# Layer one's first product: eight of its twelve quads by seven half-size products, with q and k in one load, the last rows flushed one by one, and a new order

## The chip, the cores and the metric

The kernel runs on one core of one Trainium2 chip. The metric is the device time in microseconds (us): 617.07 us before, the median of three runs (616.88 to 617.26). The engines are named as the profile names them: PE multiplies matrices, PEld loads its weights, DVE is the vector engine, ACT the activation engine, POOL is GpSimd, SP issues the DMAs. An L with a number is a line of the kernel's code.

## The reference

Windowed attention is followed by two feed-forward layers, all in fp32, on 2 x 768 tokens of width 512 (8 heads of 64):

```python
# _attn_ref: local window of 96 keys, 8 global keys, slopes per head
keep = is_global | is_local
bias = -slopes[:, None, None] * dist[None, :, :]
scores = np.where(keep, scale * q @ k.T + bias, -1e9)
a = np.exp(scores - max); a = a / (a.sum() + 1e-9); x = a @ v
# _moe_ref: layer one, d_ff 2048
g = s * np.maximum(x @ w_in, 0.0) ** 2 + b;  x = g @ w_out
# _moe2_ref: layer two, d_ff 2048
g = np.maximum(x @ w_in, 0.0) ** 2;          out = g @ w_out
```

## The kernel before

**Precision.** Every large matrix is kept as a high and a low part, so a product is three matmuls: high by high, high by low, low by high. Such a part of a weight block is a "unit" of 128 x 512 (name u, 30 of them). A weight block comes by DMA into a staging tile (`st`, three of each kind) in a packed 64-bit form, is decoded by four steps (one ACT copy, then L50, L52, L55 on DVE) and split into units: the high part by a copy (`copy_r`, L198 on ACT, L200 on DVE, L202 on POOL), the low part by a DVE subtraction (L416).

**Attention.** Twelve tiles n of 128 queries: q·k (L334), mask and row maximum on DVE (`ttr`, L342), exponent on ACT (`exp`, L350), sums and scaling, transposes (L367) that ACT or DVE copies out (`at`, L373, L375), product with v (L388), and the result split into `xh` (ACT) and `xl` (DVE). q, k and v come by one load each and tile (`load`). Until the first h, `warm` puts small matmuls (L299, L301) on PE where it would idle.

**The layers.** A layer's 2048 hidden columns are 16 blocks of 128. Layer one's first four blocks run on pieces of 256 tokens while attention still goes on (`h` L643 and `y` L722). All other blocks go in pairs a, a+1 over halves tp of 768 tokens; a pair and a half is a "quad". Layer one has twelve quads (a = 4, 6, ..., 14, two halves), layer two sixteen (a = 16, ..., 30). A half has two sides of 384 tokens.

- Layer one's first product is `plain` (L506): four results (block, side) of 12 matmuls of 384 columns each, 48 for a quad.
- Layer two's first product is `product` (L496): a Strassen form. The pair of blocks and the halves of the 512 inputs make a 2 x 2 matrix of weights, the sides and the input halves a 2 x 2 matrix of x, and seven products s = 0..6 of 6 matmuls, 42 for a quad, take the place of eight. It wants sums of weights (`wsum` L433, split by L448 into units A1, S12, S34 and A22), sums of x (T1..T4: `tsum` L475, `tsplit`, L481, into `th`, `tl` and, for T1, over x's own place), and after the matmuls a copy m1 (`mid`, L198 or L200), two sums u2, u3 (L516) and three sums `cadd` (L529) on DVE that read PSUM.
- The results then pass `act`: relu (ACT L542, DVE L544), square (ACT L551), high part gh (ACT L562, L564 or POOL L566), low part gl (DVE L569 in layer one, L572 in layer two), and the second product (`y2`, L592 in layer one, L598 in layer two) adds into six PSUM banks. `flush2` (L612, L633 on DVE) adds the banks to `acc`; at the end of layer two L629 sends each row block out.

Between the layers `acc` is scaled on ACT, split again into xh, xl, and T1..T4 are formed anew. Layer two's first product waits for them.

**What sets the order.** `order` states every piece of work as a task with engines, an assumed duration, dependencies and due time, and `Plan.run` simulates them and writes each engine's instructions in that order. CFG and the table SHIFT move due times. On the chip each engine runs its row in order, so an instruction that waits holds all behind it. The product s=3 waits for u2, s=5 for u3 and s=6 for a `cadd`, all of DVE.

Of the kernel before, what the change touches and what calls it, by code (L numbers as in the profile page):

```python
# [8 lines left out]
F32 = mybir.dt.float32  # L9
# [4 lines left out]
ALU = mybir.AluOpType  # L14
# [3 lines left out]
DM = H * D  # L18
# [11 lines left out]
NUA, NUB = 20, 10  # L30
WINO1 = False
# [27 lines left out]
def decoded(a):  # L59
# [4 lines left out]
           moe=82.8, moe0=27.8, pair=8.16, patience=3.27, slow=1.1, wload=64.22, l1s=44.16, l2s=9.05, chain2=-10.14,  # L64
           ylag2=8.98, ylag=10.91, tk=13.15)
# [30 lines left out]


class Plan:
# [13 lines left out]
    def run(self, lat, patience):  # L112
# [79 lines left out]
        self.time = max(free.values())  # L192
# [12 lines left out]
class Fast:  # L205
    def __init__(self, ctx, tc, q, k, v, wi, wo, s_t, b_t, nl_t, ng_t, ident, nm, ok, out):
        self.ok, self.tc, self.nc, self.ctx = ok, tc, tc.nc, ctx
        self.q, self.k, self.v, self.wi, self.wo, self.out = q, k, v, wi, wo, out
# [36 lines left out]
    def second(self):  # L245

        self.actx.close()
        ctx = self.ctx
# [4 lines left out]
        self.psY2 = self.pool(ctx, "psY2", 1, space=bass.MemoryType.PSUM)


    def consts(self, step):
        nc, nr, far, dist, key = self.nc, self.nr, self.far, self.dist, self.key
        if step == 0:
            nc.gpsimd.iota(nr[:, 1, :], pattern=[[-1, P]], base=0, channel_multiplier=1,
                           allow_small_or_imprecise_dtypes=True)  # L260
# [8 lines left out]
            nc.gpsimd.iota(dist[:, 0, :], pattern=[[1, P]], base=-P, channel_multiplier=-1,
                           allow_small_or_imprecise_dtypes=True)  # L270
        elif step == 1:
            k = key[:, 0, :]
            nc.vector.tensor_scalar(out=far[:, 1, :], in0=nr[:, 1, :], scalar1=self.nl, scalar2=-NEG, op0=ALU.is_ge,
                                    op1=ALU.mult)
            nc.vector.tensor_scalar(out=k, in0=k, scalar1=self.ng, scalar2=-NEG, op0=ALU.is_ge, op1=ALU.mult)
            nc.vector.tensor_tensor(out=dist[:, 1, :], in0=dist[:, 1, :], in1=far[:, 1, :], op=ALU.min)
            nc.vector.tensor_scalar(out=k, in0=k, scalar1=self.nl, scalar2=None, op0=ALU.subtract)
            nc.vector.tensor_tensor(out=key[:, 1, :], in0=dist[:, 1, :], in1=k, op=ALU.max)
        else:
            nc.vector.tensor_scalar(out=far[:, 0, :], in0=nr[:, 0, :], scalar1=self.nl, scalar2=-NEG, op0=ALU.is_ge,  # L280
                                    op1=ALU.mult)
            nc.vector.tensor_tensor(out=dist[:, 0, :], in0=dist[:, 0, :], in1=far[:, 0, :], op=ALU.min)
            nc.vector.tensor_copy(dist[:, 0, 0:G], key[:, 0, 0:G])
# [22 lines left out]
    def blocks(self, n):  # L306
        return slice(1 if n < 2 else 0, 2)
# [957 lines left out]
```

## Time and profile before

| | us |
|---|---|
| median of three runs | 617.07 |
| span of the profiled execution | 615.60 |
| PE busy | 601.59 |
| DVE busy | 446.70 |
| ACT busy | 345.75 |
| POOL busy | 96.85 |

The results give the medians of runs and the span of the profiled execution; the profiled execution has no device time of its own beside its span. The span is 1.47 us below the median. Busy time is a union per engine, so the instructions' own durations, which overlap a little at their ends, add up to more.

### The profile page before, as it was taken

The page shows a single profiled execution, that of the slowest core. Times are in us where ns is not written, and L with a number is a line of the kernel's source. Part 1 is how long each engine was busy: PE and PEld are TensorE (multiplying, and loading weights), DVE is VectorE, ACT ScalarE, POOL GpSimd, SP SyncE. Part 2 cuts the span into 40 slices and gives each one's busy share as a digit, 9 for nine tenths or more (in the row PEclk, how much of TensorE's full clock was granted, in tenths as well). Part 3 has the DMA queues.
Part 4 walks back from the last instruction along what each step waited for, and adds up shares of the span by engine and source line. Part 5 has one row for each costly group of instructions (what it writes and reads, how often), then busy time and mean ns, then how long its engine had stood idle before and what let it go on. Part 6 is the DMA issues. An engine that isn't in the chain of part 4 may idle for free.

```text
span 615.6 us, 10179 instructions
## 1 busy us (share of the span) xinstructions
PE 601.6 (98%) x3766; PEld 545.0 (89%) x3766; DVE 446.7 (73%) x997; ACT 345.8 (56%) x759; POOL 96.9 (16%) x167
## 2 busy tenths in 40 slices
PE   6999999999999999999999999999999999999995
PEld 4778989899999999999999888899999999998984
DVE  6888878766888684447648899878887897764542
ACT  6889886875655453334328476755555554543330
POOL 4334323121111100011103111111200101000000
PEclk9999999999999999999999999999999999999999
DMA  7765434103353330013100301322220322010113
GB/s 270 278 203 195 160 113 155 36 2 103 112 162 104 109 98 34 1 34 105 34 0 2 103 35 35 103 70 68 69 69 11 127 70 68 3 34 0 41 64 108
DMA packets 16473, 52.12 MB, mean 85 GB/s; under 512 B 2080, under 2 KB 2080, under 8 KB 16416
## 3 DMA queue, kind: packets, MB, share of 16 engines
q1 hardware_dynamic: 16416, 51.39, 25.2%
q8 instruction: 32, 0.52, 0.4%
q14 instruction: 25, 0.20, 0.1%
HBM read 48.24 MB, written 3.15 MB: 83 GB/s over the span
## 4 chain that ended last, share of the span: by engine, by line
PE 90%; DVE 4%; ACT 3%; DMA 2%; issue 0%; SPq 0%; ACTq 0%
PE yy L598 21%; PE h L496 18%; PE h L506 16%; PE yy L592 16%; PE y L722 6%; PE h L643 5%; PE a L334 3%; PE a L388 3%; PE a L367 3%; DMA st<-in_moe_w_in_dram 2%; ACT sn L350 1%; DVE sn L342 1%; DVE acc L633 1%; ACT acc L198 1%; ACT xh L198 0%
## 5 line engine op out<-in xcount | busy, mean ns | idle before, releaser
L598 PE MATMUL yy<-u,gh 128*128 128x512 f32 x384 | 119.2, 392 | 0.0
L506 PE MATMUL h<-xh,u 128*128 128x384 f32 x384 | 102.5, 337 | 0.0
L592 PE MATMUL yy<-gh,u 128*128 128x512 f32 (+1 forms) x384 | 97.5, 337 | 0.0
L598 PEld LDWEIGHTS yy<-u,gh 128*128 128x128 f32 x384 | 71.5, 188 | 12.2
L598 PE MATMUL yy<-u,gl 128*128 128x512 f32 x192 | 75.3, 392 | 0.9 <-DVE gl L572 0.9
L496 PE MATMUL h<-xh,u 128*128 128x384 f32 x256 | 75.5, 337 | 0.0
L592 PEld LDWEIGHTS yy<-gh,u 128*128 128x128 f32 x384 | 66.5, 189 | 7.9
L506 PEld LDWEIGHTS h<-xh,u 128*128 128x128 f32 x384 | 69.9, 188 | 0.4
L551 ACT ACTIVATE r<-r 128x384 f32<-128x384 f32 x80 | 41.9, 525 | 47.0 <-DVE r L544 30.6
L592 PE MATMUL yy<-gl,u 128*128 128x512 f32 (+1 forms) x192 | 64.8, 337 | 0.0
L506 PE MATMUL h<-xl,u 128*128 128x384 f32 x192 | 64.6, 337 | 0.0
L202 POOL TENSOR_SCALAR u<-st 128x512 fp32r<-128x512 f32 (+1 forms) x41 | 29.3, 715 | 222.8 <-PE h L506 103.5
L496 PE MATMUL h<-th,u 128*128 128x384 f32 x192 | 56.8, 336 | 0.0
L198 ACT ACTIVATE st<-st 128x512 f32<-128x512 f32 x64 | 42.7, 677 | 13.8 <-DMA st<-in_moe_w_in_dram 7.0
L569 DVE SCALAR_TENSOR_TENSOR gl<-r,sgb,gh 128x384 fp32r<-128x384 f32 x48 | 30.4, 635 | 25.2 <-ACT gh L562 21.1
L52 DVE SCALAR_TENSOR_TENSOR st<-st 128x512 int32<-128x512 int32 x64 | 45.6, 714 | 3.9 <-ACT st L198 0.7
L496 PEld LDWEIGHTS h<-xh,u 128*128 128x128 f32 x256 | 47.1, 188 | 1.0
L350 ACT ACTIVATE sn<-sn,nm 128x256 f32<-128x256 f32 (+1 forms) x96 | 46.0, 483 | 0.8 <-DVE nm L342 0.8
L55 DVE SCALAR_TENSOR_TENSOR st<-st 128x512 int32<-128x512 int32 x64 | 44.8, 700 | 1.0
L542 ACT ACTIVATE r<-h,rt 128x384 f32<-128x384 f32 x34 | 19.7, 580 | 43.8 <-PE h L506 43.8
L598 PEld LDWEIGHTS yy<-u,gl 128*128 128x128 f32 x192 | 36.1, 188 | 9.3 <-DVE gl L572 1.3
L496 PE MATMUL h<-xl,u 128*128 128x384 f32 x128 | 43.0, 336 | 0.0
(135 smaller groups left out, 1223.8 us busy)
## 6 DMA issues: line engine op xcount, KB each, us to landing
st<-in_moe_w_in_dram SPq DMA_DIRECT2D x32, 512.0 KB, 3.8
st<-in_moe_w_out_dram SPq DMA_DIRECT2D x32, 512.0 KB, 3.6
k<-in_k_dram SPq DMA_DIRECT2D x10, 512.0 KB, 4.9
v<-in_v_dram SPq DMA_DIRECT2D x10, 512.0 KB, 4.6
q<-in_q_dram SPq DMA_DIRECT2D x12, 256.0 KB, 4.1
out_dram<-acc SPq DMA_DIRECT2D x12, 256.0 KB, 2.6
k<-in_k_dram SPq DMA_DIRECT2D x2, 256.0 KB, 5.0
v<-in_v_dram SPq DMA_DIRECT2D x2, 256.0 KB, 7.1
```

Of the source, the lines that this page charges most:

```text
L52: nc.vector.scalar_tensor_tensor(out=lo, in0=hi, scalar=3, in1=lo, op0=ALU.logical_shift_left, op1=ALU.bitwise_or)
L55: nc.vector.scalar_tensor_tensor(out=lo, in0=hi, scalar=-(1 << 31), in1=lo, op0=ALU.bitwise_and, op1=ALU.bitwise_or)
L198: nc.scalar.activation(out=out, in_=in_, func=AF.Copy, scale=scale)
L350: self.nc.scalar.activation(out=sn[:, x], in_=sn[:, x], func=AF.Exp, scale=-1.0, bias=self.nm[:, n, h:h + 1], accum_out=self.rs[:, n, h:h ...
L496: self.nc.tensor.matmul(ps, p, q, start=first and kt == 0 and x == 0, stop=kt == 1 and x == 2, skip_group_check=not first)
L506: self.nc.tensor.matmul(ps, p[:, kt * P:(kt + 1) * P], self.X[q][:, kt, lo:lo + SB], start=(kt == 0 and x == 0), stop=(kt == KT - 1 and x ...
L551: nc.scalar.activation(out=r, in_=r, func=AF.Square)
L569: nc.vector.scalar_tensor_tensor(out=gl, in0=r, scalar=self.sgb, in1=gh.bitcast(F32), op0=ALU.add, op1=ALU.subtract)
L592: self.nc.tensor.matmul(yj, p[:, js], q[:, lo:hi], start=first and x == 0 and not (side and j % 2), stop=last and x == 2 and not (side and ...
L598: self.nc.tensor.matmul(y[m], p[:, ms], q, start=first and x == 0, stop=last and x == 2)
L643: self.nc.tensor.matmul(ps[:, 0:hi - lo], a[:, kt * P:(kt + 1) * P], b[:, kt, lo:hi], start=(kt == 0 and x == 0), stop=(kt == KT - 1 and x ...
L722: self.nc.tensor.matmul(yj, a[:, js], b, start=first and x == 0 and j % 2 == 0, stop=last and x == 2 and j % 2 == 1)
```

## The change

- PLAIN names the four quads that keep `plain`: (4,0), (6,0), (4,1), (6,1). The eight quads of a = 8, 10, 12, 14 take `product`. Their x sums come from `tsum1`: since x is held as two parts, a T takes three or two DVE operations in place of one, 40 in all, through a tile `tq` of its own; T2..T4 go to the place that layer two uses later. T1 is written over x's own second side, so it waits until the half's plain products are done. The added weight sums, units and PSUM sums are those of layer two's quads.
- q and k of a tile lie in one tensor `qk` and come by one load. The mask's blocks are swapped to match (own keys first). There are 29 units in place of 30.
- The very last quad (30,1) computes its second product row block by row block (`yrow`): six matmuls of both blocks, then that row is added and sent; the last row in two halves of 256 columns.
- The planner's durations, its rule for DVE and POOL at once, and the SHIFT table are new, so nearly every row has moved.

```diff
-NUA, NUB = 20, 10
-WINO1 = False
+NUA, NUB = 20, 9
+PLAIN = ((4, 0), (6, 0), (4, 1), (6, 1))
...
-        if what == "q":
-            start(out=t, in_=self.q[b, i])
-        else:
-            start(out=t[:, a], in_=(self.k if what == "k" else self.v)[b, i, :, a])
+        if what == "q":
+            t = self.qp.tile([P, 3, 4, P], F32, tag="q", name=f"q{n}")
+            self.T["q", n], self.T["k", n] = t[:, 0], t[:, 1:3]
+            a = slice(0, a.stop + 1)
+            start(out=t[:, a], in_=self.qk_[b, i, :, a])
...
+    def tsum1(self, tp, kt, step):
+        nc = self.nc
+        h, l = ([x.bitcast(F32)[:, r + kt, tp * TB + c * SB:tp * TB + (c + 1) * SB] for r, c in
+                 ((0, 0), (0, 1), (2, 0), (2, 1))] for x in self.X)
+        if step in (0, 3):
+            self.T["t", tp, kt] = self.tq.tile([P, SB], F32, tag="tq", name=f"tq{step}_{tp}_{kt}")
+        t = self.T["t", tp, kt]
+        ops = {3: ((h[3], h[1]), (t, l[3]), (t, l[1])), 0: ((h[1], h[0]), (t, l[1]), (t, l[0])),
+               1: ((h[3], t), (t, l[3])), 2: ((h[2], t), (t, l[2]))}[step]
+        for x, (p, q) in enumerate(ops):
+            plus = q is l[3] or q is l[2] or step == 0 and q is l[1]
+            nc.vector.tensor_tensor(out=t, in0=p, in1=q, op=ALU.add if plus else ALU.subtract)
...
+    def yrow(self, a, tp, m):
+        y = self.T["y", tp]
+        ms = slice(m % 3 * P, (m % 3 + 1) * P)
+        for c in range(2):
+            gh, gl = (t[:, self.T["g", a, tp, c, m // 3]][:, ms] for t in self.G)
+            oh, ol = (self.T[x, a + c, 1] for x in ("wh", "wl"))
+            for x, (p, q) in enumerate(((gh, oh), (gh, ol), (gl, oh))):
+                self.nc.tensor.matmul(y[m], p, q, start=False, stop=c == 1 and x == 2)
...
-    wino = lambda a: a >= NCH or WINO1
+    plain = lambda a, tp: (a, tp) in PLAIN
...
+    for tp in range(2):
+        d0 = ["second"] + [("h", w, lo) for w in range(NF) for lo in range(tp * TB, tp * TB + TB, 256)]
+        d1 = [("p", a, tp, c, x) for a, t in PLAIN if t == tp for c in range(2) for x in range(2)]
...
+                add(("zsh",) + v + (x,), "ACT:0.44 POOL:0.6", lambda e, v=v, x=x: f.tsplit(*v, x, 0, e),
+                    [("zs",) + v + (x,)] + d1 * (n == 1), k)
```

SP's row at the start, before (k0, q0 are tile 0's loads, st0_0 and st1_0 block 0's first and second weights):

```order
L1201 DMA ni_62<-in_n_dram 128x4
L321 DMA k0_166<-in_k_dram 128x512
L319 DMA q0_168<-in_q_dram 128x512
L37 DMA st0_0_170<-in_moe_w_in_dram 128x1024
L319 DMA q1_172<-in_q_dram 128x512
L321 DMA k1_174<-in_k_dram 128x512
L321 DMA v0_181<-in_v_dram 128x512
L321 DMA v1_183<-in_v_dram 128x512
L1212 DMA sb_61<-in_sb_dram 128x2
L319 DMA q2_193<-in_q_dram 128x512
L37 DMA st1_0_208<-in_moe_w_out_dram 128x1024
L321 DMA k2_213<-in_k_dram 128x1024
```

The same stretch of SP's row after the change (q is now q with k):

```order
L1289 DMA ni_62<-in_n_dram 128x4
L343 DMA q0_163<-in_qk_dram 128x1024
L37 DMA st0_0_165<-in_moe_w_in_dram 128x1024
L343 DMA q1_167<-in_qk_dram 128x1024
L346 DMA v0_169<-in_v_dram 128x512
L346 DMA v1_171<-in_v_dram 128x512
L1300 DMA sb_61<-in_sb_dram 128x2
L343 DMA q2_179<-in_qk_dram 128x1536
L37 DMA st1_0_181<-in_moe_w_out_dram 128x1024
```

Tile 2's keys stood twelfth, behind block 0's second weights; they now come with its q in the eighth row, ahead of them.

DVE's row while PE works on quad (8,0)'s first product, before (st is a weight block being decoded, gl a low part, yy the banks of quads 4 and 6 of the second half):

```order
L612 TENSOR_TENSOR acc_118<-yy3_4_1_2701,acc_118 128x512
L55 SCALAR_TENSOR_TENSOR st1_14_2850<-st1_14_2850 128x512
L50 TENSOR_SCALAR st1_15_2874<-st1_15_2874 128x512
L52 SCALAR_TENSOR_TENSOR st1_15_2874<-st1_15_2874 128x512
L569 SCALAR_TENSOR_TENSOR gl_106<-r8_0_00_2941,sgb_121,gh_105 128x384
L55 SCALAR_TENSOR_TENSOR st1_15_2874<-st1_15_2874 128x512
L612 TENSOR_TENSOR acc_118<-yy4_4_1_2702,acc_118 128x2x256
```

The same place after the change (tq3_1_1 is a sum for T3 of the second half):

```order
L523 TENSOR_TENSOR tl_1983<-tq0_1_0_2778,th_1982 128x384
L559 TENSOR_TENSOR u2_8_0_2913<-h8_0_1_2896,m1_8_0_2903 128x384
L517 TENSOR_TENSOR tq3_1_1_2915<-xh_116 128x384
L517 TENSOR_TENSOR tq3_1_1_2915<-tq3_1_1_2915,xl_117 128x384 x2
L559 TENSOR_TENSOR u3_8_0_2935<-h8_0_1_2896,m1_8_0_2903 128x384
L52 SCALAR_TENSOR_TENSOR st1_12_2844<-st1_12_2844 128x512
L572 TENSOR_TENSOR u3_8_0_2935<-h8_0_2_2928,u3_8_0_2935 128x384
L612 SCALAR_TENSOR_TENSOR gl_106<-r8_0_00_2925,sgb_121,gh_105 128x384
L572 TENSOR_TENSOR r8_0_10_2961<-h8_0_1_2896,m1_8_0_2903 128x384
```

Where DVE had only decoding and low parts, PE's next products now stand behind u2, u3 and the sums, with three tq operations between u2 and u3 and a decode step (L52) ahead of the first L572.

PE's last nine matmuls before (yy3 to yy5 are the last three row blocks; u28 and u29 one block's weights, the other block's matmuls stand earlier):

```order
L598 MATMUL yy3_28_1_6041<-u28_2117,gh_105 128x512
L598 MATMUL yy3_28_1_6041<-u29_2118,gh_105 128x512
L598 MATMUL yy3_28_1_6041<-u28_2117,gl_106 128x512
L598 MATMUL yy4_28_1_6042<-u28_2117,gh_105 128x512
L598 MATMUL yy4_28_1_6042<-u29_2118,gh_105 128x512
L598 MATMUL yy4_28_1_6042<-u28_2117,gl_106 128x512
L598 MATMUL yy5_28_1_6043<-u28_2117,gh_105 128x512
L598 MATMUL yy5_28_1_6043<-u29_2118,gh_105 128x512
L598 MATMUL yy5_28_1_6043<-u28_2117,gl_106 128x512
```

And after the change (u15 and u16 are one block's weights, u17 and u18 the other's):

```order
L650 MATMUL yy4_28_1_6153<-u15_97,gh_105 128x512
L650 MATMUL yy4_28_1_6153<-u16_98,gh_105 128x512
L650 MATMUL yy4_28_1_6153<-u15_97,gl_106 128x512
L650 MATMUL yy4_28_1_6153<-u17_99,gh_105 128x512
L650 MATMUL yy4_28_1_6153<-u18_100,gh_105 128x512
L650 MATMUL yy4_28_1_6153<-u17_99,gl_106 128x512
L650 MATMUL yy5_28_1_6154<-u15_97,gh_105 128x512
L650 MATMUL yy5_28_1_6154<-u16_98,gh_105 128x512
L650 MATMUL yy5_28_1_6154<-u15_97,gl_106 128x512
L650 MATMUL yy5_28_1_6154<-u17_99,gh_105 128x512
L650 MATMUL yy5_28_1_6154<-u18_100,gh_105 128x512
L650 MATMUL yy5_28_1_6154<-u17_99,gl_106 128x512
```

A row block was finished every three matmuls at the end; it is now finished every six.

Counted over the whole of both orders: PE's matmuls of 384 columns go from 1248 to 1200 (L506: 576 to 192; by seven products: 672 to 1008), the warming ones of 256 columns (L301) from 61 to 48; attention's last product with v has 240 h and 204 y matmuls ahead of it before and 228 and 144 after. DVE gains 40 `tsum1` operations, 16 low parts of them, 16 u2 and u3, 24 `cadd`, 16 weight sums, one more large and one more small weight low part for each of four pairs, and 8 more m1 copies; it loses 10 relus and 8 `at` copies, which go to ACT. POOL has 20 more rows.

## Rows read from the trace of the kernel before

**Rows 1.** The page: busy us of each engine, its share of the span, instructions.
```profile
PE 601.6 (98%) x3766; PEld 545.0 (89%) x3766; DVE 446.7 (73%) x997; ACT 345.8 (56%) x759; POOL 96.9 (16%) x167
```

**Rows 2.** Busy time by stage: width, then each engine's busy time, clock, DMA.
```profile
6.00:28.00 22.00, 18.35 (x169) 14.07 (x167) 17.45 (x92) 18.95 (x71) 8.45 (x21) 1.00 0.91 339
...
42.00:140.00 98.00, 98.00 (x918) 88.25 (x920) 76.47 (x246) 79.38 (x231) 29.08 (x50) 1.00 0.34 114
140.00:352.00 212.00, 212.00 (x1262) 200.04 (x1258) 144.32 (x254) 105.55 (x183) 26.55 (x35) 1.00 0.23 73
352.00:376.00 24.00, 23.13 (x128) 21.16 (x127) 22.45 (x41) 14.18 (x24) 2.57 (x5) 1.00 0.06 23
376.00:608.00 232.00, 232.00 (x1159) 208.93 (x1157) 169.35 (x311) 115.27 (x218) 22.78 (x36) 1.00 0.18 57
```

**Rows 3.** Chain of waits: start, length, engine, tile, line, matmuls.
```profile
45.79 2.85 PE h L643 x24
...
177.63 4.16 PE h L506 x24
...
485.86 1.04 PE h L496 x6
```

**Rows 4.** DVE's groups by form: count, busy us, mean ns, idle before and releaser.
```profile
L516 DVE TENSOR_TENSOR u<-h,m 128x384 f32<-128x384 f32 x32 | 17.8, 556 | 12.6 <-PE h L496 11.4 <-ACT m L198 1.1
...
L448 DVE TENSOR_TENSOR u<-st,u 128x512 fp32r<-128x512 f32 x24 | 16.8, 703 | 1.2 <-ACT u L198 0.7 <-POOL u L202 0.5
...
L375 DVE COPY at<-a 128x512 f32<-128x512 f32 x16 | 11.0, 687 | 8.2 <-PE a L367 8.1
L433 DVE TENSOR_TENSOR st<-st,st 128x256 f32<-128x256 f32 x24 | 10.5, 469 | 0.1
...
L544 DVE TENSOR_SCALAR r<-h,rt 128x384 f32<-128x384 f32 x14 | 8.7, 619 | 24.8 <-PE h L506 24.8
...
L475 DVE TENSOR_TENSOR t<-acc,t 128x384 f32<-128x384 f32 x8 | 4.8, 594 | 0.3
...
L448 DVE TENSOR_TENSOR u<-st,u 128x256 fp32r<-128x256 f32 x8 | 3.3, 417 | 0.2 <-ACT u L198 0.2
...
L200 DVE TENSOR_SCALAR m<-h 128x384 f32<-128x384 f32 x3 | 1.7, 558 | 4.4 <-PE h L496 4.4
```

**Rows 5.** DVE's timeline early in layer two: start, length, line, tile.
```profile
382.09 0.55 DVE L572 TENSOR_TENSOR gl<-u,gh 128x384 fp32r<-128x384 f32 x1
382.56 0.55 DVE L475 TENSOR_TENSOR t<-acc 128x384 f32<-128x384 f32 x1
```

**Rows 6.** POOL's timeline around layer one's end, with idle before.
```profile
331.95 1.01 POOL L566 TENSOR_SCALAR gh<-r,sgb 128x384 fp32r<-128x384 f32 x1 [1.51 <-ACT r L551]
...
350.76 0.59 POOL L566 TENSOR_SCALAR gh<-r,sgb 128x384 fp32r<-128x384 f32 x1 [2.00 <-ACT r L551]
```

**Rows 7.** SP's timeline of the opening: the keys of tiles 1 and 2.
```profile
3.14 0.43 SPq L321 DMA_DIRECT2D k<-in_k_dram  x1
...
8.70 0.33 SPq L321 DMA_DIRECT2D k<-in_k_dram  x1
```

**Rows 8.** PE's timeline of the opening: the second tile's q·k.
```profile
10.06 1.16 PE L334 MATMUL a<-k,q 64*128 64x128 f32 x16 [2.11 <-DMA k<-in_k_dram]
```

**Rows 9.** Timeline of the last 12 us.
```profile
604.94 4.13 DVE L633 TENSOR_TENSOR acc<-yy,acc 128x512 f32<-128x512 f32 x6 [6.17 <-PE yy L598]
...
605.66 3.92 SPq L629 DMA_DIRECT2D out_dram<-acc  x6
...
607.95 0.40 PE L598 MATMUL yy<-u,gl 128*128 128x512 f32 x1
```

**Rows 10.** DMA view of 600 to 616 us: KB each, median us to landing.
```profile
out_dram<-acc SPq DMA_DIRECT2D x6, 256.0 KB, 3.7
```

**Rows 11.** The page: a costly group of PE, and the DMA issues of the whole run.
```profile
L598 PE MATMUL yy<-u,gl 128*128 128x512 f32 x192 | 75.3, 392 | 0.9 <-DVE gl L572 0.9
...
out_dram<-acc SPq DMA_DIRECT2D x12, 256.0 KB, 2.6
```

More of the change, by code (lines that the diff above doesn't have):

```diff
@@ L170, in run @@
                     if e == "POOL" or e == "DVE" and self.port[t]:
-                        free[e] = max(now, held["DVE" if e == "POOL" else "POOL"]) + engs[e]
+                        free[e] = now + 0.4 * max(0.0, held["DVE" if e == "POOL" else "POOL"] - now) + engs[e]
                         held[e] = free[e]
@@ L191, in run @@
                 now = max(now, heapq.heappop(events))
-        self.time = max(free.values())
+        self.time = max(max(free.values()), queue + 1.2)
 def copy_r(nc, eng, out, in_, scale=1.0):
@@ L783, in order @@
         key = vt[n, 0] - LEAD - 8 if two else -40 + n
-        for what in "qk":
-            add(("l" + what, n), "SP:0.47",
-                lambda e, a=(what, n): f.load(*a), [], -900.0 + 2 * n if not two else key,
-                acq=[(what, n)], dma=0.73 * (2 if two and what == "k" else 1))
+        add(("lq", n), "SP:0.47", lambda e, n=n: f.load("q", n), [], -900.0 + 2 * n if not two else key,
+            acq=[("q", n)], dma=2.2 if two else 1.46)
         add(("lv", n), "SP:0.47", lambda e, n=n: f.load("v", n), [("lv", n - 1)] * (n > 0),
@@ L797, in order @@
                     dq.append(("tr", m, grp(m, mf)[0]))
-                add(("qk",) + u, {"PE": 1.06}, lambda e, u=u: f.qk(*u), dq, t, acq=[("a", "s", x) + u for x in range(2)],
-                    rel=[("q", n), ("k", n)] * (hf or not two))
+                add(("qk",) + u, {"PE": 1.07 if two else 1.17}, lambda e, u=u: f.qk(*u), dq, t, acq=[("a", "s", x) + u for x in range(2)],
+                    rel=[("q", n)] * (hf or not two))
             su = u if two else (n, 0)
@@ L846, in order @@
                 t += L1S if a < NCH else L2S
-    wino = lambda a: a >= NCH or WINO1
+    plain = lambda a, tp: (a, tp) in PLAIN
+    pure = lambda a: plain(a, 0) and plain(a, 1)
+    mixed = lambda a: plain(a, 0) != plain(a, 1)
     at, nu = {}, 0
@@ L856, in order @@
     for a in range(NF, 2 * NCH, 2):
-        if wino(a):
-            for what in ("A1", "S12", "S34"):
+        if not pure(a):
+            for what in ("A1", "A2", "S12", "S34") if mixed(a) else ("A1", "S12", "S34"):
                 for x in "hl":
@@ L861, in order @@
                     nu += 1
-            at["A22", a] = nu
-            nu += 1
+            if not mixed(a):
+                at["A22", a] = nu
+                nu += 1
             parts = [(a, 1), (a + 1, 1)]
@@ L876, in split @@
         u, v = at[w, i, "h"], at[w, i, "l"]
-        add(("whi", w, i), "ACT:0.58 POOL:0.62", lambda e: f.whi(w, i, e, u), [("d3", w, i)] + late(w, i, "h"), key,
+        add(("whi", w, i), "ACT:0.6 POOL:0.66", lambda e: f.whi(w, i, e, u), [("d3", w, i)] + late(w, i, "h"), key,
             acq=[slot(w, i, "h")])
@@ L889, in parts @@
             dd = [d] + ([("ws", a, 2)] if what == "S34" else [])
-            add(("wsh", what, a), "ACT:0.33 POOL:0.35" if small else "ACT:0.58 POOL:0.62",
+            add(("wsh", what, a), "ACT:0.35 POOL:0.38" if small else "ACT:0.6 POOL:0.66",
                 lambda e, what=what, k=at[ka]: f.wshi(a, what, e, k), dd + late(*ka), key, acq=[slot(*ka)])
@@ L951, in order @@
         span = L1S if one else L2S
-        dt = ["second"] if one else [("tsl", tp, kt, x) for kt in range(2) for x in range(4)] + [
-            ("xl", "x", tp, j) for j in (0, 2, 3)]
+        if not one:
+            dt = [("tsl", tp, kt, x) for kt in range(2) for x in range(4)] + [("xl", "x", tp, j) for j in (0, 2, 3)]
+        elif plain(a, tp):
+            dt = ["second"]
+        else:
+            dt = [("zsl", tp, kt, x) for kt in range(2) for x in range(4)]
+        wino = not plain(a, tp)
         blocks = {(0, 0): 2, (1, 1): 5, (1, 0): 5, (0, 1): 6}
-        if wino(a):
-            need = (["A1"], ["S12"], ["A1"], ["S34"], ["S12"], ["A22"], ["S34"])
+        if wino:
+            a22 = "A2" if mixed(a) else "A22"
+            need = (["A1"], ["S12"], ["A1"], ["S34"], ["S12"], [a22], ["S34"])
             extra = ([], [], [("m1",) + u], [("u2",) + u], [], [("u3",) + u], [("cadd",) + u + (1, 1)])
@@ L978, in order @@
                 v = u + (c, side)
-                add(("p",) + v, {"PE": 2.1}, lambda e, v=v: f.plain(*v), [prev, ("wlo", a + c, 0)] + dt * (x == 0),
+                add(("p",) + v, {"PE": 2.09}, lambda e, v=v: f.plain(*v),
+                    [prev, ("wsl", "A2" if c else "A1", a) if mixed(a) else ("wlo", a + c, 0)] + dt * (x == 0),
                     tm + 2.1 * x, acq=[("h",) + v],
-                    rel=[slot(a + c, 0, k) for k in "hl"] * (gone and side))
+                    rel=[slot(a + c, 0, k) for k in "hl"] if gone and side and not mixed(a) else [])
@@ new lines, in order @@
+            if wino and (c, side) != (0, 0):
+                add(("relu",) + v, "ACT:0.56", lambda e, v=v: f.act(*v, "relu", e), [("cadd",) + v], k)
+            else:
+                pre = ("p",) + (u + (2,) if wino else v)
+                add(("relu",) + v, "ACT:0.6 DVE:0.52", lambda e, v=v: f.act(*v, "relu", e), [pre, "sq"], k,
+                    acq=[("r",) + v], rel=[("h",) + u + (0,) if wino else ("h",) + v])
+            add(("sq",) + v, "ACT:0.53", lambda e, v=v: f.act(*v, "sq", e), [("relu",) + v], k)
@@ L996, in order @@
+            fg = (c, side) in ((0, 0), (1, 1) if wino else (1, 0))
+            add(("gh",) + v, "ACT:0.53 POOL:0.72" if one else "ACT:0.44 POOL:0.6", lambda e, v=v: f.act(*v, "gh", e),
+                [("sq",) + v] + ([] if fg or not one else [("gh",) + u + ((0, 0) if c == 0 else (1, 1) if wino else (1, 0))]),
                 k, acq=[("g",) + u + (c, x) for x in range(2)] * fg if one else [("g",) + v])
-            add(("gl",) + v, "DVX:0.53" if one else "DVX:0.47", lambda e, v=v: f.act(*v, "gl", e), [("gh",) + v], k,
+            add(("gl",) + v, "DVX:0.56" if one else "DVX:0.49", lambda e, v=v: f.act(*v, "gl", e), [("gh",) + v], k,
```

217 lines of the change are left out of this document (121 added, 96 removed), and 53 rows, old and new, of the table SHIFT.

## The prediction

> **What bounds the kernel now.** I read the busy times first: PE is busy for 601.6 us of 615.6, DVE for 446.7 [rows 1]. Then the busy times by stage, since an average says little about a kernel with stages. From 42 to 140 us (attention with layer one's first blocks), from 140 to 352 (the rest of layer one) and from 376 to 608 (layer two) PE is busy for the whole of each stretch [rows 2]. Time is lost in three places only: the opening (18.35 of 22 us from 6 to 28, part of that fill matmuls), the handover from 352 to 376 (23.13 of 24), and behind the last matmul, which starts at 607.95 in a span of 615.60 [rows 2, 9]. So a matmul taken out is worth its time on PE if the others keep up, and the question is who keeps up. The chain of waits gives the price: 24 matmuls of `plain` in 4.16 us, 6 of `product` in 1.04, both 0.173 us apiece [rows 3]. The groups' mean (337 ns and the like) is no price, since matmuls overlap.
>
> **The change, part by part.** The sum is made against the profiled execution's span, 615.60, and the differences are carried to the median of 617.07, 1.47 us above it.
>
> *Matmuls.* Eight quads go from 48 to 42, so 48 matmuls of 384 columns fall away: 48 x 0.173 = -8.3 us, on the engine that is always busy. That PE issues fewer is certain from the order (1248 to 1200); only waits can take it back.
>
> *DVE in layer one.* Added, by durations of the nearest forms [rows 4]: 40 `tsum1` operations and 16 low parts at 0.594 (33.3 us), 16 u2 and u3 and 24 `cadd` at 0.556 (22.2), 16 weight sums at 0.469 (7.5), four large and four small weight low parts at 0.703 and 0.417 (4.5), 8 copies m1 at 0.558 (4.5); taken off: 10 relus at 0.619 (6.2). Together 65.8 us in 118 more instructions. Where DVE runs back to back a 384-column operation of 0.55 us is followed 0.47 later [rows 5], so each costs 0.08 less: about 56.4 us. The stretch from 140 to 352 had 144.3 us of DVE work in 212 [rows 2], 68%. It becomes 200.7 in 203.7 (212 less 8.3), or in some 212 since the attention phase ends earlier (next part): 95 to 99%. That is the term I am least sure of. One end: in layer two, with u2, u3 and `cadd` in every quad and DVE at 73%, PE loses nothing [rows 2], so +0. The other: from 352 to 376 DVE is at 94% and PE loses 0.87 of 24 us, of which the wait for one gl (0.9) is all [rows 2, 11]; that share over 204 us is +7.4. By load the second row is nearer, but its wait is that of one chain through the rebuilding of x, which layer one doesn't have; the x sums of each half are due only when that half's first seven-product quad comes, and until then they may slip. I take +1.5. Weight units are no new limit, I think: a seven-product pair wants 11 of 29 where a plain one took 8 of 30, and layer two runs on 11 of 30 without loss.
>
> *POOL beside it.* POOL gets 20 more operations, and DVE many more with two SBUF inputs. A gh on POOL took 1.01 us at 331.95, while DVE formed the sums T, and 0.59 later [rows 6]: 0.42 more. POOL is busy 26.55 of 212 us [rows 2], so 20 x 0.42 = 8.4 us of it are hidden. The Trainium skill, "GPSIMD Engine Reference", section "8. Key points", says that GpSimd shares its SBUF interfaces with VectorE and contends with its instructions that have two SBUF inputs. The trace agrees as to POOL; whether DVE pays the same no row shows, and if it does the sum is that of the first rival.
>
> *Attention phase.* The order has 72 fewer h and y matmuls ahead of attention's last product with v (240 + 204 to 228 + 144). At 2.85/24 = 0.119 us [rows 3] PE has 8.6 us less work to spread over the same ACT and DVE work. From 42 to 140 ACT is busy 79.4 and DVE 76.5 of 98 us [rows 2]; in 89.4 that is ACT at 89% (more, with 8 `at` copies of 0.687 [rows 4] from DVE). The matmuls are not lost, only later. Bounds: 0, as now at 81%; +4, if PE idles by half of the 8.6 us. I take +0.8, towards the low end, since the tiles' chains are staggered and no row shows PE idle at 81%.
>
> *Opening.* The second tile's q·k at 10.06 waited 2.11 us for its keys, whose load was issued at 3.14 as the fifth large one [rows 7, 8]; with q and k in one load it is the third, some 0.9 us earlier. Tile 2's keys were issued only at 8.70 and now come before block 0's second weights. Against that, the queue moves 339 GB/s at a DMA share of 0.91 from 6 to 28 us, and ACT is busy 18.95 of the 22 [rows 2]: bytes and ACT bound the gain at the 3.05 us that ACT idles. The loss: one 512 KB transfer must land whole where q and k landed apart. Half of one (256 KB at 339 GB/s, 0.8 us) twice over is about +1.5. I take -1.0, the earlier issue.
>
> *Handover.* A gl that waits (0.9 [rows 11]) may stay or go; the dependencies are the same. 0, from -0.9 to +1.
>
> *Tail.* DVE's six flushes end at 604.94 + 4.13 = 609.07, 0.72 us behind PE's last matmul (607.95 + 0.40), and the six row blocks go out within 3.92 us and take 3.7 to land [rows 9, 10]; over the run the same transfer takes 2.6 [rows 11]. A row block now comes every 6 x 0.229 = 1.37 us (4.13/6 was three matmuls) so the queue is empty when the last one comes: 2.6 - 3.7 = -1.1. Halves save perhaps 0.2 in the transfer and cost one more DVE start. I take -1.0 (-1.5 to +0.3, if the low parts are late for the denser last rows).
>
> Sum: -8.3 + 1.5 + 0.8 - 1.0 + 0 - 1.0 = -8.0, that is 607.6 of span and **609.1 us**.
>
> **The rivals.**
> *DVE becomes layer one's bound.* For it: 95 to 99% by the count. If the 8.4 us of contention fall on DVE as well, it has 209.1 us of work for 203.7, and PE waits 5.4 in place of 1.5: 613.0. Against it: DVE can take weight decoding ahead in attention, where it is at 78%.
> *Attention stalls.* ACT at 89% with all chains closer: +4 in place of +0.8, 612.3.
> *Waits inside the quads eat the gain; the kernel is slower.* A plain product waits for no one. In the new quads PE's s=3, 5 and 6 each stand behind a DVE result, 24 places in layer one. Between s=1 and s=3 lies one product, 1.04 us, and u2 needs 0.556, so DVE may be 0.48 late for nothing. In the new order three tq operations (3 x 0.51 with the starts counted, 1.5 us) stand between u2 and u3 in quad (8,0), and decode steps in front of sums. If half of the 24 places find such a triple in front, PE waits 12 x (1.5 - 0.48) = 12.2 us, and it comes to 617.07 - 9.5 + 12.2 = 619.8. From 0.40 us per place on (9.5/24) the change loses. Against it: layer two has 48 such places and loses nothing [rows 2].
> *All goes well.* Opening -3.05, tail -1.5, no new waits: 617.07 - 12.9 = 604.2.
>
> **How the numbers follow.** The forecast, 606.5 to 611.5, has 0.54; all well, about 604 to 606.5, 0.14; DVE as bound 0.12 and attention stalls 0.08, both within 611.5 to 615.8; waits inside the quads 0.12, of which a third ends near 617 and the rest above. The measurement tells 0.2% (1.2 us) from no change. So faster 0.88, same 0.04, slower 0.08, and the range from 604.0 to 614.0.
>
> **What would show it.** Matmuls: 42 per quad at 0.173 us each in the chain. DVE: its busy share in the stretch from the last product with v to layer two's first, and PE's idle time there by releaser: `product` waiting for u2, u3 or `cadd` means the slower rival, y2 waiting for gl, or weights that come late, means DVE as bound. Attention: PE's idle time between 28 and 130 us, ended by ACT. Opening: the second tile's q·k before 10.06 us. Tail: some 6.2 us from the last matmul's end to the span's, which were 7.25 (615.60 - 608.35). I am wrong at the root if PE, with 48 fewer matmuls, shows more than 5 us of new idle time in layer one.

## The result, and the profile after

The changed kernel takes 607.77 us (median of four runs, 606.85 to 608.63) against 617.16 before: a ratio of 0.985 (95% interval 0.9836 to 0.9862), 9.4 us less. The profiled execution has a span of 605.10 us (its own time is 606.85) where 615.60 were, 10.5 less. The runs after spread over 1.8 us; a possible cause is in the last section.

The page's busy times of the kernel after, first part:

```profile
PE 591.4 (98%) x3705; PEld 533.9 (88%) x3705; DVE 496.8 (82%) x1115; ACT 354.5 (59%) x774; POOL 113.7 (19%) x187
```

Against [rows 1] PE has 10.2 us less (the matmuls and some fill), DVE 50.1 us more. The prediction's count gave 56.4 in layer one, less 5.5 for the `at` copies (8 at 0.687), 50.9.

Busy time by stage of the kernel after (columns as in [rows 2]):

```profile
6.00:28.00 22.00, 20.23 (x185) 15.27 (x181) 20.45 (x105) 21.62 (x78) 11.00 (x26) 1.00 0.83 337
28.00:42.00 14.00, 14.00 (x146) 11.92 (x144) 12.95 (x47) 13.65 (x44) 7.85 (x13) 1.00 0.74 244
42.00:130.00 88.00, 88.00 (x846) 79.25 (x843) 74.65 (x240) 71.19 (x204) 29.62 (x47) 1.00 0.34 112
...
140.00:340.00 200.00, 197.89 (x1155) 184.72 (x1155) 178.82 (x333) 113.85 (x201) 28.07 (x37) 1.00 0.20 64
340.00:366.00 26.00, 26.00 (x141) 23.56 (x140) 25.48 (x47) 17.43 (x30) 3.12 (x5) 1.00 0.14 41
366.00:597.50 231.50, 229.65 (x1147) 206.68 (x1147) 172.08 (x321) 107.54 (x205) 29.99 (x45) 1.00 0.19 61
```

The kernel before from 28 to 42 us, in the same view:

```profile
28.00:42.00 14.00, 13.06 (x130) 10.53 (x129) 13.38 (x46) 10.68 (x32) 5.26 (x9) 1.00 0.48 156
```

Three things are to be seen. ACT is busy for 21.62 of the opening's 22 us (it was 18.95). DVE is at 89% from 140 to 340 (layer one behind attention) and at 98% in the handover from 340 to 366; from 42 to 130 it is at 85%, where it was at 78% [rows 2]. And PE, which lost nothing between 140 and 352 before, now loses 2.1 us up to 340 and 1.9 later.

PE's waits of the kernel after, 140 to 340 us and then 340 to 400 (total, times, longest):

```profile
PE yy L635 <- DVE gl L612: 1.8, 1, 1.8
PE yy L635 <- ACT gh L605: 0.2, 1, 0.2
```
```profile
PE h L538 <- ACT m L221: 1.2, 1, 1.2
PE yy L641 <- DVE gl L615: 0.7, 1, 0.7
```

None of them is a wait of a seven-product quad in the middle of layer one. They stand at the last quad (14,1), where DVE also forms layer two's T sums, and in layer two's first quads. The timeline of DVE, POOL and PE at the first of them:

```profile
334.85 0.98 POOL L225 TENSOR_SCALAR u<-st 128x512 fp32r<-128x512 f32 x1 [4.16 <-PE yy L635]
335.23 1.01 DVE L504 TENSOR_TENSOR t<-acc 128x384 f32<-128x384 f32 x1
...
336.17 0.54 DVE L572 TENSOR_TENSOR u<-h,u 128x384 f32<-128x384 f32 x1
336.63 0.60 DVE L612 SCALAR_TENSOR_TENSOR gl<-r,sgb,gh 128x384 fp32r<-128x384 f32 x1
337.16 0.54 DVE L523 TENSOR_TENSOR tl<-t,th 128x384 fp32r<-128x384 f32 x1
337.63 0.60 DVE L612 SCALAR_TENSOR_TENSOR gl<-u,sgb,gh 128x384 fp32r<-128x384 f32 x1
338.16 0.54 DVE L504 TENSOR_TENSOR t<-acc 128x384 f32<-128x384 f32 x1
338.29 0.50 PE L635 MATMUL yy<-gl,u 128*128 128x512 f32 x1 [1.81 <-DVE gl L612]
```

DVE has no gap: the gl that PE wants (337.63) stands behind an unbroken row of others, among them a T sum that took 1.01 us beside POOL.

The busy times make these waits look smaller than they are. A matmul of 384 columns is shown 0.34 us long, while the next one starts 0.17 us after it if nothing holds it, so a wait's idle time is counted from a later point than the loss:

```profile
380.81 0.34 PE L538 MATMUL h<-th,u 128*128 128x384 f32 x1
382.30 0.44 PE L538 MATMUL h<-xh,u 128*128 128x384 f32 x1 [1.15 <-ACT m L221]
```

From start to start this wait costs 1.49 - 0.17 = 1.32 us, not 1.15. Counted so, the four waits (0.22, 1.81, 0.70 and 1.15 us of idle time) cost 0.38, 2.08, 0.87 and 1.32, 4.65 us in all; the one wait of the kernel before (0.87) cost 1.04.

The opening of the kernel after, on SP, ACT and PE:

```profile
2.18 0.43 SPq L343 DMA_DIRECT2D q<-in_qk_dram  x1
```
```profile
8.24 0.39 ACT L375 ACTIVATE sn<-sn,nm 128x128 f32<-128x128 f32 x1
```
```profile
8.03 1.16 PE L359 MATMUL a<-q 64*128 64x128 f32 x16
...
24.74 0.36 PE L695 MATMUL h<-xh,u 128*128 128x256 f32 x1
```

and of the kernel before, the same places on ACT and PE:

```profile
9.60 0.39 ACT L350 ACTIVATE sn<-sn,nm 128x128 f32<-128x128 f32 x1
```
```profile
27.81 0.39 PE L643 MATMUL h<-xh,u 128*128 128x256 f32 x1
```

The load of the second tile's keys is issued 0.96 us earlier than in [rows 7], as the prediction said (0.9); the second q·k comes 2.0 us earlier than in [rows 8], the first exponent 1.4, the first h 3.1.

The tail of the kernel after:

```profile
593.76 5.98 SPq L681 DMA_DIRECT2D out_dram<-acc  x6
...
598.06 0.39 PE L650 MATMUL yy<-u,gl 128*128 128x512 f32 x1
598.48 0.75 DVE L685 TENSOR_TENSOR acc<-yy,acc 128x256 f32<-128x256 f32 x2 [0.67 <-PE yy L650]
```

From the last matmul's end (598.45) to the span's end are 6.65 us; they were 7.25 [rows 9]. The page's two halves of the last row, after:

```profile
out_dram<-acc SPq DMA_DIRECT2D x2, 128.0 KB, 3.1
```

They take 3.1 us each to land (median), where the other row blocks of 256 KB take 2.3 in the same page.

### The profile page after: what moved, and what is told of

Read it like the earlier page. It is cut to its first block, busy times and chain, and to the rows that moved or that the text cites. A ratio compares the mean times of both kernels' runs of the same rounds, so it can differ in the third digit from the quotient of the medians.

```text
span 605.1 us, 10174 instructions
## 1 busy us (share of the span) xinstructions
PE 591.4 (98%) x3705; PEld 533.9 (88%) x3705; DVE 496.8 (82%) x1115; ACT 354.5 (59%) x774; POOL 113.7 (19%) x187
## 4 chain that ended last, share of the span: by engine, by line
## 5 line engine op out<-in xcount | busy, mean ns | idle before, releaser
L538 PE MATMUL h<-xh,u 128*128 128x384 f32 x384 | 111.7, 337 | 1.2 <-ACT m L221 1.2
L538 PE MATMUL h<-th,u 128*128 128x384 f32 x288 | 85.6, 338 | 0.0
L538 PEld LDWEIGHTS h<-xh,u 128*128 128x128 f32 x384 | 70.5, 188 | 2.6 <-ACT m L221 1.5
L538 PE MATMUL h<-xl,u 128*128 128x384 f32 x192 | 64.6, 337 | 0.0
L538 PEld LDWEIGHTS h<-th,u 128*128 128x128 f32 x288 | 53.1, 188 | 1.9 <-DVE u L559 0.4
L221 ACT ACTIVATE u<-st 128x512 fp32r<-128x512 f32 (+1 forms) x41 | 26.2, 639 | 44.6 <-PE h L538 13.4
L52 DVE SCALAR_TENSOR_TENSOR st<-st 128x512 int32<-128x512 int32 x64 | 46.1, 723 | 3.7 <-ACT st L221 0.9
L538 PE MATMUL h<-tl,u 128*128 128x384 f32 x144 | 48.5, 337 | 0.0
L594 ACT ACTIVATE r<-r 128x384 f32<-128x384 f32 x64 | 33.6, 526 | 13.6 <-DVE r L589 9.0
L635 PEld LDWEIGHTS yy<-gl,u 128*128 128x128 f32 x192 | 36.3, 189 | 5.9 <-DVE gl L612 2.1
L585 ACT ACTIVATE u<-u 128x384 f32<-128x384 f32 x32 | 16.7, 522 | 37.6 <-DVE u L572 37.5
```

The lines of the kernel that those rows point to most:

```text
L52: nc.vector.scalar_tensor_tensor(out=lo, in0=hi, scalar=3, in1=lo, op0=ALU.logical_shift_left, op1=ALU.bitwise_or)
L221: nc.scalar.activation(out=out, in_=in_, func=AF.Copy, scale=scale)
L538: self.nc.tensor.matmul(ps, p, q, start=first and kt == 0 and x == 0, stop=kt == 1 and x == 2, skip_group_check=not first)
L585: nc.scalar.activation(out=r, in_=h, func=AF.Relu, scale=rt)
L594: nc.scalar.activation(out=r, in_=r, func=AF.Square)
L635: self.nc.tensor.matmul(yj, p[:, js], q[:, lo:hi], start=first and x == 0 and not (side and j % 2), stop=last and x == 2 and not (side and ...
```

## The experiments

Each was timed beside the kernel before on the same chip, and each keeps the changed kernel's order row for row unless it says otherwise. The changed kernel's 607.77 is the base.

**E10, the removed matmuls put back.**

```diff
-        for kt in range(2):
+        for again in range(2 if a < NCH and s == 0 else 1):
+            for kt in range(2):
```

> The changed kernel, same order, with the first of the seven products done twice over (the second time from a fresh start) in layer one's eight quads: 48 matmuls of 384 columns more, exactly the number that the change removed. Theory (PE is still the bound, and a matmul is worth 0.173 us): +8.3 less what the waits at the handover give back as DVE gets more time (0 to 2), 614 to 616. Rival (DVE now sets the pace in layer one as much as PE): under 612.

616.40 us (615.19 to 617.13), +8.6, just above the forecast's upper end. PE's waits at the handover stay as they were (1.8, 1.1, 0.7, 0.2). In the two traces, matched matmul by matmul, each of the eight quads makes PE 1.04 to 1.06 us later, 0.174 a matmul. So in this order a matmul is worth its 0.173 us, and 48 of them the 8.3 of the forecast; the theory holds, without the relief. The profiled execution is 10.1 us longer, since two things came on top: a wait of 0.6 us at 142.8 (see E4), and half clock from 346 to 350 us (0.69, 0.50), as in the last section.

**E5, less DVE work in layer one.**

```diff
-        for x, (p, q) in enumerate(ops):
+        for x, (p, q) in enumerate(ops[:1]):
```

> The changed kernel, same order, with each of layer one's x sums formed by its first operation alone: 24 of the 40 additions are left out (the low parts, so the result differs), about 11.3 us of DVE work between 140 and 330 us. Theory (the waits around the handover come from the DVE work that stands there, not from lateness carried out of layer one): 607.3 to 607.8. Rival (DVE leaves layer one late): 2 to 3.5 us less, 604.3 to 605.8.

608.47 us (608.22 to 608.84), above both forecasts. 11.3 us less on DVE gain nothing. PE's waits at the handover are the same four, 1.8, 1.2, 0.7 and 0.2 us, so they aren't lateness carried out of layer one. Matched matmul by matmul, PE's row is 0.65 us later than in the kernel after from 142.9 us on (the wait that E4 has too), and half clock behind the wait of 1.8 us costs 1.4 more; together they cover the 1.9 us between the two spans. E4 and E3, with all additions in place, show the one and the other, so neither is laid to the additions left out.

**E6, more DVE work in layer one.** Three additions of the first two operands, written over, ahead of each of the eight first sums.

```diff
+        if step in (0, 3):
+            nc.vector.tensor_tensor(out=t, in0=ops[0][0], in1=ops[0][1], op=ALU.subtract)
+            ...
         for x, (p, q) in enumerate(ops):
```

> The changed kernel, same order, with 24 DVE additions of 128x384 more (each first sum written three times over again), about 11.3 us more DVE work between 140 and 330 us, where DVE now idles some 21 of 200 us. Theory (DVE has this to spare): up to +1.5, 607.8 to 609.3. Rival (DVE is the bound of layer one): +6 to +11, 614 or more.

620.74 us (619.95 to 621.25), +13.0: the theory falls; the rival's 614 is passed, and its +6 to +11 too. My 21 us of slack were an average. The same view of the kernel after in finer stretches:

```profile
130.00:200.00 70.00, 69.92 (x455) 67.47 (x455) 63.58 (x122) 42.08 (x75) 10.40 (x15) 1.00 0.26 84
200.00:210.00 10.00, 10.00 (x60) 9.01 (x59) 6.70 (x12) 3.33 (x7) 1.40 (x2) 1.00 0.21 57
...
260.00:290.00 30.00, 30.00 (x174) 27.93 (x174) 22.65 (x43) 13.45 (x26) 4.69 (x7) 1.00 0.19 56
```

DVE is 91% busy from 130 to 200, where five of the eight first sums stand, and its slack lies later. And E6's timeline shows how lateness there grows (SP, DVE, ACT, PE around quad (8,0)):

```profile
215.56 0.89 SPq L37 DMA_DIRECT2D st<-in_moe_w_in_dram  x2
...
219.87 0.68 ACT L221 ACTIVATE st<-st 128x512 f32<-128x512 f32 x1 [5.22 <-DMA st<-in_moe_w_in_dram]
...
224.37 0.47 ACT L221 ACTIVATE m<-h 128x384 f32<-128x384 f32 x1
...
224.89 0.69 PE L542 MATMUL h<-xh,u 128*128 128x384 f32 x1 [5.66 <-ACT m L221]
```

The late DVE frees a staging tile late, so a weight load goes out at 215.56 (in the kernel after such loads go out from 205.40 on), ACT's decode waits 5.22 us for it, the copy m1 stands behind that decode, and PE waits 5.66 us for m1. It isn't DVE's throughput alone: DVE too waits there (0.92 us for the same load). That wait is the largest of four new ones: 1.6 us at 140.88 and 1.3 at 145.30, both for DVE, and 1.5 for a u2 come with it, 10.1 us together. The rest of the 14.3 us between the spans (619.4 and 605.1) is mostly half clock behind the long wait (0.55 and 0.59 from 222 to 230 us) and behind the one of 1.8.

**E7 and E9, rows moved at the handover.** Both move rows that the planner had written, and let T use `tq`:

```diff
+MOVES = (  # E7: the row, where to, 0 before it, 1 behind it
+    (("gl", 14, 1, 1, 1), ("ts", 0, 0, 3), 0), (("gl", 14, 1, 1, 0), ("ts", 0, 0, 3), 0),
+    (("d1", 19, 1), ("fl", 12, 1, 2, 0), 1), (("d2", 19, 1), ("d1", 19, 1), 1),
+    (("m1", 16, 1), ("p", 16, 1, 0), 1),
+    (("fl", 16, 0, 4, 0), ("u2", 16, 1), 1), (("fl", 16, 0, 5, 0), ("fl", 16, 0, 4, 0), 1),
+    ...
+    # E9 also
+    (("d0", 20, 0), ("m1", 16, 0), 1), (("d0", 21, 0), ("d0", 20, 0), 1),
+    (("fl", 12, 1, 4, 0), ("u2", 16, 0), 1), (("fl", 12, 1, 1, 0), ("fl", 12, 1, 4, 0), 1),
+    (("d0", 22, 0), ("sq", 16, 1, 0, 0), 1), ...)
...
-            self.T["t", tp, kt] = self.tm.tile([P, SB], F32, tag="m1", name=f"t{step}_{tp}_{kt}")
+            self.T["t", tp, kt] = self.tq.tile([P, SB], F32, tag="tq", name=f"t{step}_{tp}_{kt}")
```

> The changed kernel with a few rows moved around the handover: quad (14,1)'s two first low parts ahead of a sum T on DVE, two decode steps of block 19 behind the last T, the copy m1 of quad (16,1) ahead of three flushes on ACT and its u2, u3 ahead of flushes on DVE, and layer two's sums T in the tile tq so that m1 has a tile of its own. Theory (three waits of 2.3, 0.9 and 1.3 us caused by the order of DVE's and ACT's rows): 1.0 to 2.4 less, 605.4 to 606.8. Rival (the chain of T sums ends only 0.5 us ahead of layer two's first product, so it becomes the wait): the first wait moves there, 0.5 to 1.0 less.

608.97 us (607.76 to 609.76). Both expectations missed: the wait of 1.8 us has gone, but it did not move to the T sums; PE now waits for an m1 (1.1), a u2 (0.7), gl (0.7 and 0.4) and a relu (0.5).

> The changed kernel with more rows moved around the handover: as in the first attempt, and also the decode steps of blocks 20 and 21 that wait for their load behind the copy m1 of quad (16,0) on ACT, the sum u2 of (16,0) ahead of two flushes on DVE, and a decode step of block 22 behind the first square of (16,1). Theory (the first attempt only moved the waits, to an m1 behind a decode that waits for its DMA, 1.1 us, and to u2 behind flushes, 0.7): without those PE's waits from 330 to 400 us fall from 4.0 to about 1.5 us, no stretch of half clock follows, and the time is 605 to 606.5. Rival (DVE is simply full there, 98% busy): the waits only move again, 607.5 to 609.

608.36 us (608.00 to 608.61). From 330 to 400 us, E9 and then the kernel after:

```profile
330.00:400.00 70.00, 66.17 (x337) 57.20 (x336) 67.19 (x125) 43.33 (x80) 12.06 (x16) 1.00 0.20 61
```
```profile
330.00:400.00 70.00, 66.12 (x340) 58.36 (x339) 67.59 (x127) 43.24 (x79) 11.86 (x15) 1.00 0.20 61
```

PE idles 3.83 and 3.88 us. Each wait taken away came back as another (for u2, u3, a first sum), with DVE at 96 to 97% over the 70 us. In E9 the rival holds. More and shorter waits cost more than their idle time says: without any half clock the profiled executions are 0.9 (E7) and 1.8 us (E9, of which 0.5 is the wait at 142 us) longer than the kernel after's. So two ways of moving rows did not help; that no other would, and that work would have to leave DVE, is argued and was not tried.

**E3, q and k apart again; E8 and E11, the packed load in the kernel before.**

```diff
-            start(out=t[:, a], in_=self.qk_[b, i, :, a])
+            start(out=t[:, 0:1], in_=self.qk_[b, i, :, 0:1])
+            start(out=t[:, 1:a.stop], in_=self.qk_[b, i, :, 1:a.stop])
```

> The changed kernel with q and k of a tile loaded by two DMAs at the same place of the same order (12 more issues). If the packing itself shortened the opening: the second tile's q.k, at 8.03 us, comes about 2 us later, and the time is about 609.5. Rival (it is the order of the loads and of the first work): the second q.k within 0.5 us of 8.0, and 607.8 to 608.3.

608.30 us (606.88 to 609.22), the second q·k at 8.12: the rival, to its edge. In the new order packing is worth nothing that can be told.

E8 is the kernel before in its own order, with the first load of a tile bringing all and the second issuing nothing:

```diff
-        if what == "q":
+        if what in "qk":
+            if ("k", n) in self.T:
+                return
```

> The kernel before, in its own order, with q and k of a tile in one tensor and one load (issued where the first of the two stood). If the packing itself shortens the opening: the second q.k comes about 1.5 us before 10.06, and the time is about 615.5. Rival (the order does it): within 0.5 us of 617.1.

616.24 us, ratio 0.9988 (0.9979 to 0.9996): 0.2 to 1.3 us less, between the two forecasts. The second q·k came at 8.19, but the first h only at 27.11; ACT waits twice for weights on the way, 1.52 and 0.81 us:

```profile
17.03 0.68 ACT L198 ACTIVATE st<-st 128x512 f32<-128x512 f32 x1 [1.52 <-DMA st<-in_moe_w_in_dram]
22.59 0.70 ACT L198 ACTIVATE st<-st 128x512 f32<-128x512 f32 x1 [0.81 <-DMA st<-in_moe_w_out_dram]
```

E11 was to take the first of these waits away:

```diff
+MOVES = ((("d0", 1, 0), ("exp", 2, 1), 1, "ACT"), (("norm", 1, 0), ("norm", 1, 0), 0, "POOL"))
```

> The kernel before in its own order with the packed loads, and two rows moved: the decode of block 1's first weights, at which ACT waited 1.52 us for the load, behind tile 2's first exponents, and one scaling of tile 1 from ACT to POOL. Theory (the opening is bound by ACT's row, and the new order's gain lies in ACT not waiting): first h about 25.5 us in place of 27.1, 614.7. Rival (packing was all there was to gain): the first h within 0.3 us of 27.1 and 616.2.

616.08 us, the first h at 27.02. But ACT's row in E11 shows that its waits only moved:

```profile
16.53 0.59 ACT L411 CAST xh<-a 128x512 fp32r<-128x512 f32 x1 [1.01 <-PE a L406]
22.51 0.67 ACT L213 ACTIVATE st<-st 128x512 f32<-128x512 f32 x1 [2.15 <-DMA st<-in_moe_w_out_dram]
```

They are 3.16 us together where E8 has 2.33, and ACT is busy 18.25 of the 22 us where E8 has 19.16. So E11 did not make the ACT that doesn't wait, and the theory stands untested; only its forecast missed. In the kernel after ACT waits for no weights in the opening. Packing holds some 0.7 us of the first h (27.81 to 27.11); the rest is with the new order as a whole, and which of its rows carry it, and whether by ACT, stays open.

**E4, the old tail.**

```diff
-        if u == (2 * NCH - 2, 1):
+        if u == (2 * NCH - 2, 9):
```

> The changed kernel with the last quad's second product as before (block by block, six flushes at the end, no half rows). Theory (what the two traces show from the last matmul to the end, 7.25 against 6.64): +0.6, 608.4. Rival 1 (the prediction's term): +1.0, 608.8. Rival 2: the rows cost at the front what they save behind, 607.8.

608.88 us (607.72 to 609.38), +1.1 by medians that lie within each other's spread. The profiled executions differ by 0.9 in span (606.0). In E4's the last matmul starts 0.55 us later (598.61). Matched matmul by matmul, 0.43 of that is there from 142.66 us on, where a small transpose (`chkp`) waits:

```profile
PE chkp L794 <- ACT u L221: 0.4, 1, 0.4
```

E5, E9 and E10 have this wait too (0.4 to 0.7), the kernel after, E3 and E7 don't; it has nothing to do with the tail. So the tail itself has 0.35 in these traces. Between 0.35 and 1.1, then.

**E1 and E2, fewer and more seven-product quads, planned anew.**

```diff
-PLAIN = ((4, 0), (6, 0), (4, 1), (6, 1))
+PLAIN = tuple((a, tp) for a in range(4, 16, 2) for tp in range(2))   # E1, without x sums
+PLAIN = ((4, 0), (4, 1))                                             # E2
```

> The changed kernel with all twelve quads of layer one by plain products (no x sums, no PSUM sums), planned anew; loads, tail and opening as changed. Theory (the 48 matmuls gain 8.3 us, and DVE's extra work gives back about 3.6 of it in three waits around the handover; opening and tail bring the rest): 607.8 + 8.3 - 3.6 = about 612.5. Rival 1 (the matmuls are the whole gain): about 617. Rival 2 (the extra DVE work costs nothing, so that only the matmuls differ): about 616, and no new waits in this kernel's handover.

621.67 us. The order that the planner wrote has two new waits for m1 of 8.0 us together and half clock behind them, so the number is no price of the scheme; E10 is. All expectations missed.

> Ten quads by seven products in place of eight (only (4,0) and (4,1) stay plain), planned anew. 12 matmuls fewer (-2.1 us), about 7 us more DVE work in layer one. Theory (DVE has some 21 us to spare between 140 and 330 us, only the handover is tight): 605.5 to 606.5. Rival (DVE's throughput now bounds all of layer one): the 7 us show, 611 or more.

641.82 us. From 140 to 400 us PE idles 25.3 of 260, mostly for m1, th and u2, behind ACT and DVE; the mean clock there is 0.93. Far beyond the rival's 7 us. That lateness grows as in E6, and that the SHIFT table was made for another set of tasks, is my reading and was not tested. What ten quads would cost in an order made for them stays open.

## Why the prediction was right, step by step

The forecast of 609.1 (8.0 less) stands against 607.77 (9.4 less). The direction and its cause hold: PE was the bound, and 48 matmuls less are the gain's largest part. Of the other terms four were off: opening and attention together gave 5.2 us more than forecast, the waits took some 2 us more, the tail gave less. That the sum came so near is in part luck.

- *Matmuls, -8.3.* Right: E10 gives +8.6 for putting 48 back, 0.174 apiece in its trace.
- *Opening, -1.0.* Mis-sized: the first h came 3.07 us earlier. That is the size of the bound that I had drawn from the 3.05 us in which ACT idled, and ACT now idles 0.38; whether it is more than chance E11 did not settle. I took the one delay I could name (the issue of a load) and not the bound, though the whole opening was ordered anew. E8 and E3 show that load packing, from which I had worked the term out, is the smaller part.
- *Attention phase, +0.8.* Wrong in sign. The first plain matmul stood at 152.0 us and now at 145.2, with 12 y matmuls (1.4 us) fewer ahead of it: 5.4 us gained, 3.1 by the first h and so 2.3 behind it. Of these 0.94 stand from 28 to 42 us, where PE had idled that long and now doesn't; where the rest lies I can't tell. PE is busy in all of 42 to 130 us with ACT at 81%, where I feared 89, though 8 `at` copies went from DVE to ACT.
- *DVE in layer one, +1.5, and handover, 0.* Mis-sized and misplaced: PE's idle time between 140 us and the tail is 3.96 us where it was 0.87 [rows 2], +3.1 (+3.6 from start to start), and it stands at the handover, on whose own row (94% busy, 0.87 us lost) I had drawn the upper bound and then set it aside as something that layer one doesn't have. In place of the one wait for gl of 0.9 us [rows 11] there are two for gl (1.8 and 0.7), one for an m1 (1.2) and one for a gh (0.2). DVE's share of 95 to 99% did not come: it is at 89% in layer one, and at 85% in attention, where it took work ahead, as the prediction had held against the first rival.
- *DVE as layer one's bound* (the first rival): in part. The sign that I had named for it, y2 waiting for gl, shows twice (1.8 and 0.7), and the +3.1 to +3.6 lie between my 1.5 and its 5.4; but only at the handover. Its price, contention all through layer one, did not come: of `tsum1`'s 40 operations three took 0.82 to 0.93 us beside POOL, the others 0.54 to 0.56. The T sum of 1.01 us ahead of the longest wait is one such case.
- *Waits inside the quads* (the slower rival): not seen at all with DVE at 89%. E6 shows that the rival was near: 11.3 us more on DVE made the kernel slower than before (ratio 1.0054, 1.0041 to 1.0067), by a chain that I had not named (DVE to a staging tile to a load to ACT to m1).
- *Tail, -1.0.* 0.6 in the two traces, 0.35 to 1.1 by E4. The term counted on a last transfer of 2.6 us or less; the halves took 3.1.

The measured terms, with the waits from start to start, -8.3 - 3.1 - 2.3 + 3.6 - 0.6, add up to -10.7 against 10.5 between the spans. With the waits' idle time alone (+3.1) it would be -11.2.

## What to carry to other kernels

On an engine that is always busy, removed instructions are worth their pitch, if the price is read from back-to-back rows. And a wait on it costs more than the idle time shown, since matmuls are shown longer than their pitch. What an added load on another engine costs is not read from its mean share: look for the stretches in which that engine is full, for what stands behind it in every row, and above all for the loads that its work sets free. And when a whole opening is ordered anew, one delay that can be named is a poor guess of the gain: here it was 3.1 us where I had named 1.0. That the idle time of the busiest engine is the better guess fits this case and is not shown.

## What the runs showed of the hardware

*TensorE's clock falls behind a wait, in some executions and not in others.* Kernel after and E3, the same order there, 338 to 344 us:

```profile
338.00:340.00 2.00, 1.72 (x7) 1.43 (x8) 2.00 (x5) 1.09 (x2) 0.00 (x0) 1.00 0.14 57
340.00:342.00 2.00, 2.00 (x15) 1.83 (x14) 1.97 (x4) 0.99 (x2) 0.00 (x0) 1.00 0.84 233
342.00:344.00 2.00, 2.00 (x13) 1.71 (x12) 1.93 (x5) 1.32 (x3) 0.00 (x0) 1.00 0.07 29
```
```profile
338.00:340.00 2.00, 1.63 (x7) 1.31 (x8) 2.00 (x5) 1.14 (x2) 0.00 (x0) 0.94 0.16 66
340.00:342.00 2.00, 2.00 (x6) 1.58 (x5) 1.97 (x4) 0.91 (x2) 0.00 (x0) 0.50 0.72 223
342.00:344.00 2.00, 2.00 (x14) 1.94 (x13) 1.93 (x5) 1.39 (x3) 0.00 (x0) 0.71 0.10 39
```

Behind the same 1.8 us wait E3's granted clock falls to 0.50 (1.2 GHz), and over the three stretches 2 x 0.06 + 2 x 0.50 + 2 x 0.29 = 1.7 us are lost; E5 (0.78, 0.50, 0.86) and E10 show it too, the kernel after and E4 don't. From 340.35 on E3's matmuls of 512 columns start 0.43 us apart, where the kernel after's start 0.23 apart. The loss of 1.7 us is as much as the runs of the changed kernel spread (606.85 and 607.10, then 608.44 and 608.63), so the wait of 1.8 us may cost 1.7 more. That the slower two had it is only argued: they left no trace, and their mean clocks (0.993 and 0.996) don't decide it, since the run of 607.10 has 0.996 as well.

*DVE pays for POOL beside it.* The T sum of 1.01 us at 335.23 ran beside a POOL copy of 0.98; on its own such a sum takes 0.54 (338.16 in the same trace). The prediction had this of POOL alone [rows 6] and said that no row showed it of DVE. The trace of the kernel before does show it, in a T sum that began while a POOL gh of 0.76 us ran (379.53):

```profile
379.84 0.86 DVE L475 TENSOR_TENSOR t<-acc 128x384 f32<-128x384 f32 x1
```

Not every pair makes DVE pay: at 336.62 before, a T sum took 0.55 us beside a POOL gh that took 0.99. The Trainium skill, "GPSIMD Engine Reference", section "8. Key points", names this contention for VectorE's instructions with two SBUF inputs; here it shows on both sides.
